# New durations in the planner that orders a fused attention and MLP kernel

## The chip, the cores and the metric

The kernel runs on one core of a Trainium2 chip. The metric is the device time of one execution in microseconds (us), and lower is better. TensorE is called PE here and its weight loads PEld; VectorE is DVE, ScalarE is ACT, GpSimd is POOL, and SyncE, which issues the DMAs, is SP.

## The reference, cut to what matters

```python
# q, k, v: 4 batches x 8 heads x 576 tokens x 64, float32
scores = (q @ k.T) / 8
thresh = scores.max(-1) - tau
scores = where(scores >= thresh, scores, -1e9)
attn   = exp(scores - scores.max(-1))
attn   = attn / (attn.sum(-1) + 1e-9)
x = (attn @ v)             # laid out as 2304 tokens x 512
h = x @ w_in               # 512 -> 2048            (first MLP)
x = (h * sigmoid(h)) @ w_out   # 2048 -> 512
out = ((x @ w_a) * (x @ w_b)) @ w_out2   # 512 -> 1536 -> 512   (second MLP)
```

## The kernel before

The work is cut into tasks, and a planner (class `Plan`) puts them in order. Every task has an engine, a cost in ns, a rank (lower goes first), tasks that it needs, and buffers that it takes from rings of a given size. The planner runs a clock of its own: whenever an engine is idle it gives it the ready task of lowest rank, and a task becomes ready when those that it needs have ended by their costs plus a lag (`LAG`, and `MORE` by the engine that receives). The order that comes out is written down, engine by engine, and on the chip each engine works through its list in that order and waits where something is not there yet. The costs do nothing else: no instruction depends on them but one kind, the fills (below).

**Attention** is 144 tiles of 128 query rows in 32 groups: for each batch and each pair of heads a group of four tiles (256 tokens, buffer `pa`) and one of five (320 tokens, `pb`). A tile runs: scores on PE into `sa` or `sb` (L516, L523); `lowest` on DVE (L532, the scaled copy and its minimum); `threshold` on DVE (L538, L540); `exp` on ACT (L544, L546); `mask` on DVE with the row sum (L549); four or five transposes on PE (L581) into `tp` or `hb`; and copies out of PSUM on ACT (L588). Per group follow the value products on PE (L626) into `av`, and a copy on ACT into `x` (L647). The row sums go out to DRAM and come back (L651, L658), GpSimd divides piece by piece (L661), and the result is stored (L665). There is one buffer `x`, so the copy L647 of a group waits for the store L665 of the group before. The first 16 tiles ("early") keep their scores in PSUM; from tile 54 on, q and k are first split in two parts (L441 on ACT, L444 on DVE, L447 on POOL).

**Weights of the first MLP** come as 32 chunks of raw words, which are put together in seven steps: two casts on ACT (L343, L348), two operations on DVE (L354, L359), an addition (L364, four pieces on POOL in the first 16 chunks, DVE after), a cast on ACT (L368) and a subtraction on DVE (L372). One buffer `wc` and two `wt`, `wraw` hold one to two chunks at a time.

**The first MLP** is 112 units: 5 blocks of 256 tokens with 16 units each and 2 blocks of 512. A unit is 12 matmuls up (L754) into PSUM bank `hb`, a tanh on ACT (L764), a gate on DVE (L767), two halves (L770 on ACT, L773 on DVE), and 12 matmuls down (L814), one unit later. Its rank is 1000 and more, so it fills what attention leaves of PE. From the sixty-sixth unit on, once attention has ended, a second bank `hc` takes every other unit; until then a unit can only begin when the gate of the one before has freed `hb`. Where PE waits before a transpose, the planner writes fills: transposes of the identity (L579), as many as 0.6 of its planned gap divided by 109 ns, at most 16.

**Weights of the second MLP** are prepared once attention has ended (lines 877 to 912, rank 1e6, so they take what is left of ACT and DVE); then the second MLP runs (L1127, L1213).

Of the kernel before, what the change touches and what calls it, by code (L numbers as in the profile page):

```python
# [20 lines left out]
B, H, S, D = 4, 8, 576, 64  # L21
# [8 lines left out]
NH = S // 2  # L30
# [26 lines left out]
R_T, R_AV, R_EV, R_NORM = 2, 3, 1, -2  # L57
# [21 lines left out]
class Plan:  # L79
# [8 lines left out]


    LAG = {"PE": 200, "DVE": 125, "ACT": 140, "Pool": 70, "none": 0}  # L90
    MORE = {"PE": 110, "Pool": 40}

    PIPE, LAND = 330, 1300
    WINDOW = 3413
# [108 lines left out]
def act_ns(n, psum=False, scalar=False):  # L203
    return int(n / 1.2 + (50 if psum else 93) + (93 if scalar else 0))


def dve_ns(n, fast=False):
    return int(n / (1.92 if fast else 0.96) + 67)


def pool_ns(n):
    return int(2.35 * n + 90)


def pieces(n, most):
# [5 lines left out]
def pe_ns(n):  # L221
    return int(n * 0.4375 + 7)
# [3 lines left out]
def fused_kernel(ctx: ExitStack, tc: tile.TileContext, qk, qk2, v, tau, w_in, w_out, w_a, w_b, w_o2, out):  # L226
# [10 lines left out]
    pl = Plan()  # L237
# [58 lines left out]
    scale = const.tile([P, 1], F32, name="scale")  # L296
# [30 lines left out]
    wt, w_ready = {}, {}  # L327

    def split_weight(key, src, rank, dst, after=(), lo_engine="Pool", scale_engine="DVE", most=512, total_engine="Pool"):
# [5 lines left out]
        s = {}  # L335
# [34 lines left out]
        def lo(o):  # L370
# [2 lines left out]
                              op=ALU.subtract)  # L373

        a = dma(rank, P * 4096, load, take=["wraw"], behind=after)
        l = pl.add("ACT", act_ns(512), rank, low, [a], take=["wt"])
        c = pl.add(scale_engine, act_ns(512) if scale_engine == "ACT" else 335, rank, scale, [a], take=["wc"],
                   port=scale_engine == "DVE")
        h = pl.add("DVE", 335, rank, sign, [a, c], port=True)
        j = pl.add("DVE", dve_ns(512), rank, join, [h, c], port=True)  # L380
# [31 lines left out]
    def add(engine, cost, rank, fn, after=(), take=(), behind=(), **kw):  # L412
        t = pl.add(engine, cost, rank, fn, after, take, behind, **kw)
        att_tasks.append(t)
        return t
# [54 lines left out]
    def inverses(n, m):  # L470

        s = {}

        def guard():
            nc.vector.tensor_scalar(out=s["sum"][:, :m], in0=s["sum"][:, :m], scalar1=EPS, scalar2=None, op0=ALU.add)

        def inverse():  # L480
            nc.vector.reciprocal(out=sums[:, :m], in_=s["sum"][:, :m])

        def total(k):
            def fn():
                if "sum" not in s:
                    s["sum"] = sm_p.tile([P, 5], F32, name="sum", bufs=2)
                return s["sum"][:, k:k + 1]
            return fn

        def finish(masked):  # L490
            gd = add("DVE", 150, n + R_NORM, guard, masked)
            return add("DVE", 150, n + R_NORM, inverse, [gd], ["rs"])

        return total, finish

# [2 lines left out]
    def softmax(parts, total):  # L498
# [4 lines left out]
        s = {}  # L503
# [46 lines left out]
                                           op0=ALU.is_ge if early else ALU.is_le, op1=ALU.mult, accum_out=total())  # L550
            s["e"] = s["e"].rearrange("p a n -> p (a n)")

        cost = 4 * pe_ns(NH) * len(parts) if parts[0][0]["split"] else 780
        s["scored"] = add("PE", cost, n, scores, [t for hd, *_ in parts for t in hd["ready"]], [bank])
        lw = add("DVE", dve_ns(S) + 75, n, lowest, [s["scored"]], ["e"] if early else ["e", "t"])
        th = add("DVE", 190, n - 0.5, threshold, [lw])
        ex = add("ACT", act_ns(S, early, True) + 30, n, exp, [lw])
        s["ready"] = add("DVE", dve_ns(S) + (110 if early else 80), n - 1, mask, [ex, th], port=not early)
        if early:
            pl.free(bank, s["ready"])  # L560
        else:
# [6 lines left out]
    def weigh(b, half, c, tiles, v, last):  # L568
# [53 lines left out]
        def values(ks):  # L622

            for k in ks:
                for h in range(2):
                    nc.tensor.matmul(s["av"][h * D:(h + 1) * D, :nq], lhsT=v["v"][:, h, k], rhs=s["p"][:, k, h * nq:(h + 1) * nq],  # L626
                                     start=(k == 0), stop=(k == 4), skip_group_check=True)
# [8 lines left out]

        av = ts
        for ks in AV_PARTS:
            av = add("PE", 2 * len(ks) * (int(nq / 1.2) + 47) + 100, last_n + R_AV, lambda ks=ks: values(ks),
                     [*(left if 4 in ks else full), v["ready"]], behind=[av])  # L640
        pl.free(buf, av)
        if last:
# [716 lines left out]
```

## Time and profile before

| | us |
|---|---|
| three runs: lowest, median, highest | 1123.73, 1124.1, 1127.24 |
| the profiled execution, its own time | 1128.0 |
| its span, first to last instruction | 1125.9 |
| PE busy (matmuls) | 1095.8 |
| DVE busy | 832.2 |
| ACT busy | 571.4 |
| POOL busy | 160.9 |

Busy shares are of the whole span. They say little by themselves, since the stages differ: attention with weight preparation up to about 200 us, attention beside the first MLP up to about 500 us, the rest of the first MLP up to about 690 us, then the second MLP. A matmul's time in the trace is from its start until its result is there; matmuls overlap, so what one takes of PE is the distance from its start to that of the next.

### The profile page before, as it was taken

The page shows a single profiled execution, that of the slowest core. Times are in us where ns is not written, and L with a number is a line of the kernel's source. Part 1 is how long each engine was busy: PE and PEld are TensorE (multiplying, and loading weights), DVE is VectorE, ACT ScalarE, POOL GpSimd, SP SyncE. Part 2 cuts the span into 40 slices and gives each one's busy share as a digit, 9 for nine tenths or more (in the row PEclk, how much of TensorE's full clock was granted, in tenths as well). Part 3 has the DMA queues.
Part 4 walks back from the last instruction along what each step waited for, and adds up shares of the span by engine and source line. Part 5 has one row for each costly group of instructions (what it writes and reads, how often), then busy time and mean ns, then how long its engine had stood idle before and what let it go on. Part 6 is the DMA issues. An engine that isn't in the chain of part 4 may idle for free.

```text
span 1125.9 us, 19426 instructions
## 1 busy us (share of the span) xinstructions
PE 1095.8 (97%) x7086; PEld 979.4 (87%) x7086; DVE 832.2 (74%) x1722; ACT 571.4 (51%) x1012; POOL 160.9 (14%) x306
## 2 busy tenths in 40 slices
PE   8889989999999999999999999999999999999998
PEld 6557857899888888899988888899999999999998
DVE  7878998777777777748998987766884668536664
ACT  6877776667666676646665654411242114401132
POOL 2443111333422243312000000000000000000000
PEclk9989999999999999999999999999999999999999
DMA  5654642323322232128998789798889888888882
GB/s 185 202 168 146 187 159 71 119 78 95 104 81 76 82 98 82 34 69 265 300 316 268 258 270 346 258 298 255 253 310 308 251 260 246 281 281 254 254 254 76
DMA packets 114975, 222.27 MB, mean 197 GB/s; under 512 B 8112, under 2 KB 75328, under 8 KB 114880
## 3 DMA queue, kind: packets, MB, share of 16 engines
q1 hardware_dynamic: 114736, 221.03, 61.5%
q8 instruction: 56, 0.92, 0.3%
q14 instruction: 39, 0.32, 0.1%
q10 hardware_dynamic: 144, 0.00, 0.0%
HBM read 173.74 MB, written 47.26 MB: 196 GB/s over the span
## 4 chain that ended last, share of the span: by engine, by line
PE 62%; DMA 0%; ACT 0%; DVE 0%; POOL 0%; issue 0%; ACTq 0%
PE pr L1127 23%; PE pr L1213 12%; PE hb L754 7%; PE hc L754 5%; PE sb L814 4%; PE yd L814 2%; PE yc L814 2%; PE yf L814 2%; PE ye L814 2%; PE av L626 1%; PE tp L581 1%; PE sa L516 1%; DMA xT_d<-x 0%; DVE tm L1072 0%; PE av L631 0%; ACT pb L588 0%
## 5 line engine op out<-in xcount | busy, mean ns | idle before, releaser
L1127 PE MATMUL pr<-w 128*128 128x384 f32 x1512 | 262.8, 334 | 0.0
L1127 PEld LDWEIGHTS pr<-w 128*128 128x128 f32 x1512 | 262.3, 188 | 0.2
L754 PE MATMUL hb<-xh,w 128*128 128x256 f32 (+1 forms) x704 | 156.2, 313 | 1.8 <-DVE th L767 1.2
L532 DVE TENSOR_SCALAR_CACHE_REDUCE t<-sa,nscale 128x576 f32<-128x576 f32 x128 | 103.7, 810 | 53.5 <-PE sa L516 46.7
L1213 PE MATMUL pr<-zh,w 128*128 128x384 f32 x504 | 128.3, 336 | 0.0
L549 DVE SCALAR_TENSOR_TENSOR e<-t,thr,e 128x576 f32<-128x576 f32 x128 | 109.8, 859 | 20.4 <-ACT e L546 18.9
L754 PEld LDWEIGHTS hb<-xh,w 128*128 128x128 f32 x704 | 114.4, 192 | 11.2 <-issue 1.6
L581 PE MATMUL tp<-ident,e 128*128 128x128 f32 x706 | 107.4, 279 | 17.0 <-DVE e L549 8.2
L581 PEld LDWEIGHTS tp<-ident,e 128*128 128x128 f32 x706 | 79.2, 141 | 41.6 <-issue 16.1
L546 ACT ACTIVATE e<-t,min 128x576 f32<-128x576 f32 x128 | 99.9, 782 | 19.5 <-DVE t L532 18.7
L754 PE MATMUL hb<-xl,w 128*128 128x256 f32 (+1 forms) x352 | 107.4, 305 | 0.7 <-POOL xl L723 0.7
L814 PE MATMUL sb<-gh,w 128*128 128x256 f32 (+1 forms) x576 | 98.6, 301 | 0.0
L1213 PEld LDWEIGHTS pr<-zh,w 128*128 128x128 f32 x504 | 91.1, 188 | 0.0
L814 PEld LDWEIGHTS sb<-gh,w 128*128 128x128 f32 x576 | 80.4, 190 | 6.6 <-issue 2.9
L1213 PE MATMUL pr<-zl,w 128*128 128x384 f32 x252 | 84.7, 336 | 0.0
L1139 ACT COPY yo<-pr 128x384 f32<-128x384 f32 x18 | 8.6, 480 | 123.4 <-PE pr L1127 123.4
L754 PEld LDWEIGHTS hb<-xl,w 128*128 128x128 f32 x352 | 67.3, 191 | 3.7 <-POOL xl L723 0.9
L516 PE MATMUL sa<-sp 128*128 128x288 f32 (+1 forms) x400 | 70.4, 302 | 0.0
L661 POOL TENSOR_TENSOR x<-x,xi 128x128 f32<-128x128 f32 (+2 forms) x80 | 41.6, 544 | 190.3 <-DMA xi<-r_d 88.9
L978 ACT CAST zh<-z 128x768 fp32r<-128x768 f32 x45 | 37.6, 836 | 61.1 <-PE pr L1213 38.7
L588 ACT COPY pb<-tp 128x512 f32<-128x512 f32 (+2 forms) x128 | 59.8, 493 | 11.9 <-PE tp L581 11.2
L447 POOL TENSOR_TENSOR sp<-qk,sp 64x115 fp32r<-64x115 f32 (+1 forms) x100 | 58.0, 611 | 52.2 <-issue 36.6
(142 smaller groups left out, 1977.6 us busy)
## 6 DMA issues: line engine op xcount, KB each, us to landing
w<-wab_d SPq DMA_DIRECT2D x126, 512.0 KB
w<-wo_d SPq DMA_DIRECT2D x63, 512.0 KB
wab_d<-uw SPq DMA_DIRECT2D x18, 896.0 KB
qk<-qk SPq DMA_DIRECT2D x20, 576.0 KB
wo_d<-uw SPq DMA_DIRECT2D x10, 896.0 KB
wraw<-w_in SPq DMA_DIRECT2D x16, 512.0 KB
wraw<-w_out SPq DMA_DIRECT2D x16, 512.0 KB
v<-v SPq DMA_DIRECT2D x20, 320.0 KB
```

Source lines behind the costliest of these rows:

```text
L447: nc.gpsimd.tensor_tensor(out=s["t"][D:, 0, o], in0=s["r"][D:, o], in1=s["t"][D:, 0, o].bitcast(F32), op=ALU.subtract)
L516: nc.tensor.matmul(s["s"][:r + m, j, :NH], lhsT=hd["t"][:, 0, c - r:c + m], rhs=hd["t"][:, k, j * NH:(j + 1) * NH], start=(k == 1), stop=( ...
L532: nc.vector.tensor_scalar(out=s["t"], in0=s["s"][:, :, :NH], scalar1=nscale, scalar2=None, op0=ALU.mult, op1=ALU.min, accum_out=s["min"])
L546: nc.scalar.activation(out=s["e"], in_=s["t"], func=AF.Exp, scale=-1.0, bias=s["min"])
L549: nc.vector.scalar_tensor_tensor(out=s["e"], in0=s["s"][:, :, :NH] if early else s["t"], scalar=s["thr"], in1=s["e"], op0=ALU.is_ge if ear ...
L581: nc.tensor.transpose(t["tp"][:, j * P:(j + 1) * P], e["e"][:, o:o + P], ident)
L588: nc.scalar.copy(out=dst(s["p"]), in_=t["tp"][:, :m * P] if m < 4 else t["tp"].rearrange("p (k q) -> p k q", k=4))
L661: nc.gpsimd.tensor_tensor(out=s["x"][:, o], in0=s["x"][:, o], in1=s["i"][:, o], op=ALU.mult)
L754: nc.tensor.matmul(s["h"], lhsT=w[:, a, o:o + P], rhs=xx, start=(c == 0 and k == 0), stop=(c == NC - 1 and k == 2))
L814: nc.tensor.matmul(ys[j][e // per][:, e % per * tn:(e % per + 1) * tn], lhsT=w[:, a, e * P:(e + 1) * P], rhs=gs[j, f][g], start=(f == 0 an ...
L1127: nc.tensor.matmul(bank[:, m, :TN], lhsT=w["w"][:, 2 * m + k, a], rhs=y[i][x][:, k, :TN], start=(i in (1, 6, 5) and k == 0 and q == 0), st ...
L1213: nc.tensor.matmul(bank[:, c, :TN], lhsT=w["w"][:, 2 * e + c, a], rhs=z[x][:, e], start=(i in (1, 6, 5) and sl == 0 and e == 0 and q == 0) ...
```

## The change

Ten numbers that the planner reckons with are replaced. No instruction of the kernel is changed by hand, and no rank, ring or lag but `MORE["Pool"]`.

```diff
-    MORE = {"PE": 110, "Pool": 40}
+    MORE = {"PE": 110, "Pool": 110}
...
 def pool_ns(n):
-    return int(2.35 * n + 90)
+    return int(2.5 * n + 95)
...
-        l = pl.add("ACT", act_ns(512), rank, low, [a], take=["wt"])
-        c = pl.add(scale_engine, act_ns(512) if scale_engine == "ACT" else 335, rank, scale, [a], take=["wc"],
+        l = pl.add("ACT", 565, rank, low, [a], take=["wt"])
+        c = pl.add(scale_engine, 565 if scale_engine == "ACT" else 335, rank, scale, [a], take=["wc"],
...
-            gd = add("DVE", 150, n + R_NORM, guard, masked)
-            return add("DVE", 150, n + R_NORM, inverse, [gd], ["rs"])
+            gd = add("DVE", 100, n + R_NORM, guard, masked)
+            return add("DVE", 90, n + R_NORM, inverse, [gd], ["rs"])
...
-        cost = 4 * pe_ns(NH) * len(parts) if parts[0][0]["split"] else 780
+        cost = 4 * pe_ns(NH) * len(parts) if parts[0][0]["split"] else 850
...
-        th = add("DVE", 190, n - 0.5, threshold, [lw])
-        ex = add("ACT", act_ns(S, early, True) + 30, n, exp, [lw])
-        s["ready"] = add("DVE", dve_ns(S) + (110 if early else 80), n - 1, mask, [ex, th], port=not early)
+        th = add("DVE", 126, n - 0.5, threshold, [lw])
+        ex = add("ACT", 725 if early else 680, n, exp, [lw])
+        s["ready"] = add("DVE", dve_ns(S) + 77, n - 1, mask, [ex, th], port=not early)
...
-            av = add("PE", 2 * len(ks) * (int(nq / 1.2) + 47) + 100, last_n + R_AV, lambda ks=ks: values(ks),
+            av = add("PE", 2 * len(ks) * (int(nq / 1.2) + 3) + 90, last_n + R_AV, lambda ks=ks: values(ks),
```

In ns this makes of the old costs: a raw cast (`act_ns(512)`) 519 to 565; a POOL piece of 128 columns 390 to 415; guard 150 to 100 and inverse 150 to 90; scores of an unsplit tile 780 to 850; threshold 190 to 126; early exp 653 to 725, late exp 696 to 680; early mask 777 to 744, late mask 747 to 744; the value products of a group of 256 columns 2800 to 2340, and of 320 columns 3330 to 2870.

What this does to the lists is shown at three places. The first is DVE's list from its thirty-first mask (L549) on, in the stage in which weights are still put together (L354, L359, L364, L372 are weight steps, L767 and L773 belong to the first MLP). Before:

```order
L549 SCALAR_TENSOR_TENSOR e,sum<-t,thr,e 128x576
L532 TENSOR_SCALAR t,min<-sa,nscale 128x576
L372 TENSOR_TENSOR w<-wt,w 128x512
L354 TENSOR_SCALAR wraw<-wraw 128x512
L540 TENSOR_SCALAR thr<-min,tadd 128x1
L359 SCALAR_TENSOR_TENSOR wc<-wc,wraw 128x512
L549 SCALAR_TENSOR_TENSOR e,sum<-t,thr,e 128x576
L364 ISA wt<-wc,wt 128x1024
L532 TENSOR_SCALAR t,min<-sa,nscale 128x576
L372 TENSOR_TENSOR w<-wt,w 128x512
L767 SCALAR_TENSOR_TENSOR th<-th,hb 128x256
L354 TENSOR_SCALAR wraw<-wraw 128x512
```

The same place, from the thirty-first mask on, in the changed kernel's list of DVE:

```order
L549 SCALAR_TENSOR_TENSOR e,sum<-t,thr,e 128x576
L773 TENSOR_TENSOR gl<-th,gh 128x256
L540 TENSOR_SCALAR thr<-min,tadd 128x1
L532 TENSOR_SCALAR t,min<-sa,nscale 128x576
L549 SCALAR_TENSOR_TENSOR e,sum<-t,thr,e 128x576
L540 TENSOR_SCALAR thr<-min,tadd 128x1
L532 TENSOR_SCALAR t,min<-sa,nscale 128x576
L549 SCALAR_TENSOR_TENSOR e,sum<-t,thr,e 128x576
L372 TENSOR_TENSOR w<-wt,w 128x512
L354 TENSOR_SCALAR wraw<-wraw 128x512
L540 TENSOR_SCALAR thr<-min,tadd 128x1
L359 SCALAR_TENSOR_TENSOR wc<-wc,wraw 128x512
```

Weight steps moved back against attention. Over the whole list the seventeenth chunk is ready (L372) after 29 masks before and after 35 now, and the last after 43 before and 48 now.

The second place is ACT's list around the copy L647 of the twenty-seventh group (128x384, that is 256 tokens and the sums). Before:

```order
L588 COPY pa<-tp 128x256
L764 ACTIVATE th<-hb 128x256
L546 ACTIVATE e<-t,min 128x576
L770 CAST gh<-th 128x256
L647 COPY x<-av 128x384
L588 COPY pb<-tp 128x4x128
L441 CAST sp<-qk 128x1152
L588 COPY pb<-tp 128x4x128
L588 COPY pb<-tp 128x256
```

The same copy, with what stands around it, in the changed kernel's list of ACT:

```order
L588 COPY pa<-tp 128x256
L770 CAST gh<-th 128x256
L546 ACTIVATE e<-t,min 128x576
L441 CAST sp<-qk 128x1152
L546 ACTIVATE e<-t,min 128x576
L647 COPY x<-av 128x384
L588 COPY pb<-tp 128x4x128 x2
L588 COPY pb<-tp 128x256
```

The cast L441 and one more exp moved ahead of the copy that waits for the `x` buffer; the copies out of `tp` behind it stayed.

The third place is DVE's list after attention's last mask, where the first MLP runs on alone (L836 empties the sums of a block; L883 to L909 prepare weights of the second MLP; `hc` in place of `hb` shows the second bank). Before, from the last two gates of small units on the one bank:

```order
L767 SCALAR_TENSOR_TENSOR th<-th,hb 128x256
L773 TENSOR_TENSOR gl<-th,gh 128x256
L767 SCALAR_TENSOR_TENSOR th<-th,hb 128x256
L773 TENSOR_TENSOR gl<-th,gh 128x256
L836 TENSOR_SCALAR yo<-sb 128x512
L767 SCALAR_TENSOR_TENSOR th<-th,hc 128x256
L773 TENSOR_TENSOR gl<-th,gh 128x256
L767 SCALAR_TENSOR_TENSOR th<-th,hb 128x256
L883 TENSOR_SCALAR ur<-ur 128x512
```

A part of the same stretch, between two gates on the one bank, in the changed kernel's list of DVE:

```order
L767 SCALAR_TENSOR_TENSOR th<-th,hb 128x256
L901 TENSOR_TENSOR us<-us 128x256
L888 SCALAR_TENSOR_TENSOR us<-us,ur 128x512
L773 TENSOR_TENSOR gl<-th,gh 128x256
L897 TENSOR_TENSOR us<-us 128x128
L894 ISA us<-us 128x1024
L897 TENSOR_TENSOR us<-us 128x128
L901 TENSOR_TENSOR us<-us 128x256
L767 SCALAR_TENSOR_TENSOR th<-th,hb 128x256
```

Attention ends earlier in the list: in PE's order 732 up matmuls (61 units) stand ahead of its last value product before, and 630 (52 and a half units) now. The second bank still begins with the sixty-sixth unit, so 12 units on one bank follow attention now, against 4, and weight steps stand between the last seven of their gates, where none stood before.

## Rows read from the trace of the kernel before

**Rows 1.** Five stretches: busy us and instructions of each engine, granted clock, DMA.
```profile
0.00:100.00 100.00, 83.81 (x555) 55.77 (x556) 80.10 (x215) 74.31 (x138) 40.53 (x90) 0.95 0.58 175
100.00:150.00 50.00, 48.76 (x363) 38.31 (x363) 48.01 (x117) 39.91 (x81) 6.91 (x12) 1.00 0.58 178
150.00:200.00 50.00, 45.83 (x343) 33.93 (x342) 40.42 (x109) 33.72 (x70) 7.08 (x12) 1.00 0.31 101
200.00:500.00 300.00, 295.95 (x2388) 264.29 (x2387) 218.67 (x614) 196.89 (x381) 96.99 (x175) 0.99 0.26 81
500.00:1126.00 626.00, 621.49 (x3446) 587.15 (x3444) 445.05 (x669) 226.55 (x346) 9.36 (x19) 1.00 0.82 266
```

**Rows 2.** PE's waits, 0 to 200 us: us in total, times, longest.
```profile
PE tp L581 <- DVE e L549: 8.2, 10, 1.9
PE sa L523 <- DVE t L532: 4.1, 7, 1.5
PE tp L581 <- ACT pb L588: 3.3, 3, 1.5
```

**Rows 3.** ACT's waits, 0 to 200 us, for the weights.
```profile
ACT w L368 <- DVE wt L364: 6.8, 9, 2.3
ACT w L368 <- POOL wt L364: 4.8, 8, 1.7
```

**Rows 4.** Timeline of DVE: start, us, instruction, count; in brackets idle before it.
```profile
104.34 0.21 DVE L540 TENSOR_SCALAR thr<-min,tadd 128x1 f32<-128x1 f32 x1
104.47 0.68 DVE L364 CUSTOM_DVE_ANT_0 wt<-wc,wt 128x1024 uint16<-128x1024 uint16 x1
```

**Rows 5.** Timeline of POOL, four pieces of one chunk.
```profile
61.03 1.69 POOL L364 TENSOR_TENSOR wt<-wc,wt 128x128 uint32<-128x128 uint32 x4 [3.94 <-DVE wc L359]
```

**Rows 6.** Timelines of ACT, SP, POOL and PE, 184 to 200 us.
```profile
184.06 0.53 ACT L647 COPY x<-av 128x448 f32<-128x448 f32 x1 [1.01 <-PE av L626]
187.03 0.51 SPq L658 DMA_DIRECT2D xi<-r_d  x1
192.57 1.66 POOL L661 TENSOR_TENSOR x<-x,xi 128x106 f32<-128x106 f32 x3 [11.69 <-DMA xi<-r_d]
194.26 0.33 SPq L665 DMA_DIRECT2D xT_d<-x  x1
198.19 0.48 ACT L647 COPY x<-av 128x384 f32<-128x384 f32 x1 [2.68 <-DMA xT_d<-x]
199.21 0.44 PE L581 MATMUL tp<-ident,e 128*128 128x128 f32 x2 [1.20 <-ACT pb L588]
```

**Rows 7.** Waits of ACT and of PE, 200 to 500 us.
```profile
ACT x L647 <- DMA xT_d<-x: 18.5, 8, 4.3
PE tp L581 <- ACT pb L588: 4.1, 3, 1.9
```

**Rows 8.** Timeline of ACT and PE at 311 us, and the stretch behind it.
```profile
310.82 0.48 ACT L647 COPY x<-av 128x384 f32<-128x384 f32 x1 [4.32 <-DMA xT_d<-x]
311.84 0.33 PE L581 MATMUL tp<-ident,e 128*128 128x128 f32 x1 [1.94 <-ACT pb L588]
312.90:316.30 3.40, 3.40 (x17) 3.40 (x17) 2.64 (x6) 2.15 (x4) 2.58 (x5) 0.50 0.10 33
```

**Rows 9.** Timeline: a unit of the first MLP on one bank, attention over.
```profile
497.02 0.28 PE L754 MATMUL hb<-xl,w 128*128 128x256 f32 x1
497.75 0.42 DVE L767 SCALAR_TENSOR_TENSOR th<-th,hb 128x256 f32<-128x256 f32 x1 [1.56 <-ACT th L764]
498.58 0.40 PE L754 MATMUL hb<-xh,w 128*128 128x256 f32 x2
```

**Rows 10.** Timeline: a unit on two banks beside weight preparation.
```profile
543.10 0.28 PE L754 MATMUL hb<-xl,w 128*128 128x256 f32 x1
544.36 1.08 DVE L909 TENSOR_TENSOR uw<-us,uw 128x896 fp32r<-128x896 f32 x1
545.36 0.41 DVE L767 SCALAR_TENSOR_TENSOR th<-th,hb 128x256 f32<-128x256 f32 x1
```

## The prediction

> **What bounds the kernel now.** I read three views in this order. First the table of stretches [rows 1]: PE is busy in nearly all of the time, and what is left, its idle time, lies in front: 16.2 us before 100 us, 1.2 and 4.2 us in the next two stretches, 4.05 us in the 300 us after them, and 4.5 us in the last 626 us, nearly all of it the store behind the last matmul. The change can't touch what PE has to compute (it orders the same matmuls, the fills apart), so all that it can win is some 25 us of PE's idle time, and all that it can lose is new idle time. From 500 us on PE stands so densely that nothing is to be had there. Second the waits of PE before 200 us [rows 2]: it waits for masks (8.2 us), for the score bank to come free (4.1 us) and for copies out of PSUM (3.3 us), never for DMA. These are links of the softmax chain on DVE and ACT. Third the waits of PE from 200 to 500 us [rows 7]: three waits of together 4.1 us, all for the copy out of `tp`, and above them ACT's eight waits of together 18.5 us in L647, for the one `x` buffer. So two things hold PE up: before 200 us the softmax chain and the weights share DVE and ACT, and after it the round of the `x` buffer sometimes stops ACT in front of a copy that PE needs.
>
> **The numbers themselves.** Each engine's list is fixed, so a cost that is wrong shows as a wait of one engine for another that the plan thought done. The threshold takes 0.13 us of DVE from its start to the next start [rows 4], not 190 ns, and a POOL piece 0.41 us (1.69 us for four, the last one counted whole, [rows 5]), not 390 ns. The new numbers are nearer for an undisturbed instruction. They are not the durations of a disturbed one: three pieces of 106 columns took 1.66 us at 192.57 us [rows 6], where the new formula says 360 ns each, together 1.08.
>
> The Trainium skill ("SBUF — State Buffer", section "Who interferes with whom") says that a DVE operation with two SBUF inputs and a GpSimd operation that reads SBUF exclude each other for a whole instruction. The 1.66 us agree with it. By that rule the corrected piece is right only between masks, and the plan stays short wherever both run; this gives the rival "no gain" below.
>
> **First term, the fills.** The order has 87 fills in place of 80. At the 109 ns that the kernel itself divides by, that is 7 x 0.109 = +0.8 us if all lie on PE's path, and 0 if each only fills a wait. I take +0.8.
>
> **Second term, before 200 us.** ACT waits 6.8 + 4.8 us for weight chunks that DVE and POOL haven't added up yet [rows 3]; behind the waiting cast stand exps and copies that PE needs. The plan thought a chunk ready too soon: 2 x 46 ns for the casts, 4 x 25 ns for the pieces and 70 ns of lag, some 0.26 us in each of the 16 chunks with POOL pieces. Now it knows, and weight steps stand later: the last chunk comes after 48 masks, not 43. That evens the load. DVE is busy 48.0 of 50 us from 100 to 150 us and 40.4 of 50 after it [rows 1], since the weights run out there, while PE waits in both. Counted in the two orders by start-to-start times, DVE has in the five groups from the seventh to the eleventh 18, 24, 15, 21 and 7 us of work before, and 15, 16, 20, 19 and 19 us now; PE has 90 us of work over these groups in both. I take it that half of PE's 5.4 us of idle time between 100 and 200 us goes, -2.5 us rounded, and of the 16.2 us before it, where both orders place 67 fills in planned gaps, only -1.0. Together -3.5 us. The bounds: at best two thirds of the waits of [rows 2] go, 15.6 x 2/3 = -10 us; at worst DVE, now loaded evenly beside PE, makes the 100 us stretch 5 us longer, +5 us (DVE's 88.4 us of work in it become 93 with the weight steps that moved in from before, and each engine waits for the other).
>
> **Third term, 200 to 500 us.** Between the value products of a five-tile group and those of the next four-tile group PE's order now holds about 12.0 us of work (20 transposes, 24 score and 34 MLP matmuls, 10 value products with two passes each) where it held 11.2, and on the other half 12.5 where it held 16.2. The round of the `x` buffer took 14.1 us at its late example: from the copy at 184.06 over the load at 187.03, the pieces at 192.57 and the store at 194.26 to the next copy at 198.19, for which ACT waited 2.68 us and PE behind it 1.20 us [rows 6]. On the half that waits now the plan leaves 0.8 us more, so each of the three waits of [rows 7] shrinks by about 0.7 us: -2.0 us. Of what is queued behind the stopped copy, a cast of the heads and an exp have moved ahead of it; the copies for PE remain. Bounds: all of 4.1 us and the slow stretch below gone, -5.8 us; on the other side two late rounds now also stop the half that was cut from 16.2 to 12.5 us, 2 x (14.1 - 12.5) = +3 us.
>
> At 312.90 us a stretch of 3.4 us ran at a granted clock of 0.50, which is 1.2 of the two levels 1.2 and 2.4 GHz, with PE busy throughout; ahead of it ACT had waited 4.32 and PE 1.94 us [rows 8]. It cost half of its length, 1.7 us. I count it only in the bound.
>
> The Trainium skill ("TensorE: Matmul & The Clock Gate", section "What's actually happening") has the slow level as the default that activity releases. The row agrees, slow right behind a wait. By the rule the stretch goes with the wait, and the third term would be -3.7, not -2.0.
>
> **Fourth term, the first MLP alone on one bank.** The last matmul up of a unit started at 497.02 us, its gate ended at 498.17, and the next unit began at 498.58 without a wait [rows 9]: 0.41 us of slack, as only 12 matmuls down stand between. Weight preparation can eat that. With two banks the gate at 545.36 us came behind a subtraction of 1.08 us and ended 2.67 us after the last matmul up at 543.10 [rows 10]; on one bank the next unit would have begun 2.67 - 1.56 = 1.1 us late. That is the latest of the 15 units from 505 to 546 us; four of them end past the slack, 0.12 us on the mean of 15. The new order has seven gates on one bank among weight steps: 7 x 0.12 = +0.9 us, between 0 and 7 x 1.1 = +7.7.
>
> **Sum.** +0.8 - 3.5 - 2.0 + 0.9 = -3.8 us. Against the profiled execution's own 1128.0 us (2.1 us outside its span) that is 1124.2. This execution lies 3.9 us above the median of the runs, so I set the difference against the median: 1124.1 - 3.8 = 1120.3 us.
>
> **The rivals.** *No gain.* The waits are set by what the new numbers leave out (collisions, DMA rounds), and only places change. For it: the 1.66 us of [rows 6], and that a DMA round, not a repriced cost, lies behind ACT's 18.5 us. Against it: the 11.6 us of [rows 3] are just what was mispriced. Second and third term go, the rest stays: 1124.1 + 1.7 = 1125.8.
>
> *Slower: the one `x` buffer becomes the bound.* Both halves of a pair now have 12.0 to 12.5 us of PE work, against a round of 14.1 us at its longest. If six of the 22 rounds after 200 us are that late and none is hidden, they cost 6 x 1.75 = +10.5 us, and the time is 1120.3 + 10.5 = 1131. It decides once rounds are longer than 12.5 us as a rule. Against it: only three PE waits in 300 us so far, and DVE has 81 us of slack there [rows 1].
>
> *Slower: DVE bounds 100 to 200 us.* The second term is then +5 in that stretch in place of -2.5, 1120.3 + 7.5 = 1128. Against it: PE's work beside it is no larger.
>
> **How the numbers follow.** A measurement of this kernel tells about 0.3% (3.4 us) from no change; faster means under 1120.7. Chances: a gain as summed 0.44, with its own range 1112 to 1120.7; no gain 0.35; the `x` buffer 0.13; DVE 0.08. So faster 0.44, same 0.35, slower 0.21. The range goes down to 1112 (second and third term halfway to their best ends) and up to 1130, which leaves out most of the `x` buffer case.
>
> **What would show it.** Right: ACT's waits in L368 before 200 us fall under 6 us, PE's idle time from 100 to 200 us to about 3 us; PE's waits for `pb` copies after 200 us total under 3 us; attention's last value product comes some 25 us earlier; between it and the second bank a few waits of PE for the gate L767, under 2 us. Wrong: ACT's waits in L647 grow past 25 us with PE waits behind them, or DVE is busy over 96% from 100 to 200 us while PE's idle time there grows.

## The result: 0.7% slower

The changed kernel takes 1133.26 us (median of 4 runs, 1132.11 to 1133.34), the kernel before 1123.91 on the same chip (4 runs, 1122.91 to 1127.24). The ratio of the comparison is 1.0068, with a 95% interval of 1.0042 to 1.0094; the quotient of the two medians, 1.0083, lies inside it. The forecast was 1120.3, within 1112 to 1130, so both the direction and the range were wrong. The profiled executions lie only 5.2 us apart (spans 1131.1 and 1125.9 us), because that of the kernel before is 4.1 us above its median. The traces can explain these 5.2 us, not all of the 9.4 between the medians. A second pair of traces with the same orders (e13 and e5 below) lies 6.6 us apart.

The table of stretches of the changed kernel answers to [rows 1] (from and to, length, then busy us and instructions of PE, PEld, DVE, ACT, POOL, the granted clock, DMA). Its last row ends 5.1 us before this kernel does; in the kernel before it runs to the end.

```profile
0.00:100.00 100.00, 86.27 (x564) 56.19 (x565) 82.16 (x222) 74.21 (x137) 39.79 (x83) 0.95 0.59 174
100.00:150.00 50.00, 46.84 (x354) 36.78 (x354) 42.05 (x110) 37.90 (x77) 10.30 (x22) 1.00 0.52 158
150.00:200.00 50.00, 45.55 (x319) 33.32 (x316) 43.01 (x106) 34.96 (x69) 6.01 (x9) 0.93 0.41 126
200.00:500.00 300.00, 296.81 (x2381) 262.86 (x2380) 230.88 (x627) 203.57 (x390) 112.48 (x193) 0.99 0.30 94
500.00:1126.00 626.00, 626.00 (x3481) 591.49 (x3481) 437.35 (x660) 223.01 (x339) 0.00 (x0) 1.00 0.81 259
```

Two rows matter. From 150 to 200 us PE begins 319 matmuls where it began 343, and its granted clock is 0.93, not 1.00. From 100 to 150 us DVE is busy 42.05 us in place of 48.01, and PE is busy 1.9 us less: DVE was relieved, and PE gained nothing.

The busy time itself misleads here. Over the whole span PE is busy 6.4 us more than before (1095.8 us), and its idle time fell from 30.1 to 28.9 us, although the kernel is slower. The busy times of the changed kernel over its whole span:

```profile
PE 1102.2 (97%) x7093; PEld 981.0 (87%) x7093; DVE 836.4 (74%) x1722; ACT 573.7 (51%) x1012; POOL 168.6 (15%) x306
```

The one row over the stretch that decides, 150 to 250 us, first of the kernel before:

```profile
150.00:250.00 100.00, 95.83 (x744) 78.46 (x743) 77.59 (x212) 67.23 (x133) 25.05 (x43) 1.00 0.33 105
```

The same stretch of the changed kernel:

```profile
150.00:250.00 100.00, 93.25 (x683) 74.01 (x679) 81.76 (x213) 68.32 (x132) 25.92 (x41) 0.95 0.37 117
```

To compare kernels I worked out PE's lost time: from each matmul's start to the next, less that distance where the same shape runs densely (119.5 ns for 128x256, 233 for 512 columns, and so on); fills and slow clock count as lost. Before, 62.1 us in all; after, 67.3. The difference is the 5.2 us of the spans. This measure sees what the idle time does not: matmuls that count as busy but stand further apart, or run at the slow clock.

What ACT waited for at the two casts of a weight chunk, 0 to 200 us, in the changed kernel ([rows 3] has the two L368 rows of before):

```profile
ACT wt L343 <- DMA wraw<-w_in: 9.6, 7, 3.2
ACT wt L343 <- DMA wraw<-w_out: 5.5, 6, 3.0
ACT w L368 <- DVE wt L364: 3.5, 4, 1.4
ACT w L368 <- POOL wt L364: 2.1, 3, 1.4
```

The rows at L343 in the kernel before, same stretch:

```profile
ACT wt L343 <- DMA wraw<-w_in: 3.9, 4, 1.2
ACT wt L343 <- DMA wraw<-w_out: 0.5, 2, 0.4
```

The waits at L368 fell from 11.6 to 5.6 us, as forecast. But those for the raw words at L343 rose from 4.4 to 15.1. Together these two waits take 20.7 us of ACT in place of 16.0 (22.4 and 19.4 with L343's waits for DVE, 1.7 us after and 3.4 before). Two of the waits for raw words and what stood behind them, first on ACT, then SP, then PE (start, us, instruction; in brackets the idle time before it):

```profile
161.02 0.66 ACT L343 ACTIVATE wt<-wraw 128x512 uint32<-128x512 uint32 x1 [1.72 <-DMA wraw<-w_in]
163.40 0.78 ACT L546 ACTIVATE e<-t,min 128x576 f32<-128x576 f32 x1
165.82 0.67 ACT L343 ACTIVATE wt<-wraw 128x512 uint32<-128x512 uint32 x1 [1.64 <-DMA wraw<-w_in]
...
161.48 0.33 SPq L665 DMA_DIRECT2D xT_d<-x  x1
161.91 0.37 SPq L339 DMA_DIRECT2D wraw<-w_in  x1
...
165.50 0.77 PE L581 MATMUL tp<-ident,e 128*128 128x128 f32 x5 [1.47 <-DVE e L549]
167.78 0.79 PE L754 MATMUL hb<-xh,w 128*128 128x256 f32 x2 [0.78 <-DVE w L372]
```

The exp L546 stood behind the waiting cast, the mask behind the exp, and the transposes L581 behind the mask; at 167.78 us a unit of the first MLP waits for its chunk. From there PE runs slowly although it has work. The whole slow stretch, and the part of it in which PE has no gap:

```profile
167.10:173.90 6.80, 5.90 (x22) 3.02 (x24) 6.80 (x18) 4.97 (x9) 0.00 (x0) 0.50 0.32 106
171.00:174.00 3.00, 3.00 (x14) 1.42 (x12) 3.00 (x7) 1.83 (x3) 0.00 (x0) 0.52 0.24 96
```

A granted clock of 0.50 is the lower of the two levels (1.2 GHz). The last chunk is ready (end of L372) at 191.8 us; before, at 177.1. At 210 us a second round stops ACT in front of PE's copies, the reload of `qk`. The chain of waits that ends there (start, us, what):

```profile
203.89 0.92 POOL sp L447
204.82 0.02 issue
204.83 4.06 DMA qk<-qk
208.89 0.02 issue
208.91 1.15 ACT sp L441
```

The copy for PE behind that cast, and PE's wait for it:

```profile
210.28 0.85 ACT L588 COPY pb<-tp 128x256 f32<-128x256 f32 x2
210.70 0.33 PE L581 MATMUL tp<-ident,e 128*128 128x128 f32 x1 [2.04 <-ACT pb L588]
```

PE loses 2.04 us, and slow clock follows here too:

```profile
211.50:214.90 3.40, 3.40 (x14) 1.48 (x13) 2.58 (x7) 1.23 (x3) 1.90 (x4) 0.50 0.12 39
```

From 150 to 250 us the kernel before ran at a clock of 1.00 throughout. The lost time that falls into these two slow stretches is 5.7 us, most of the 8.6 us by which the changed kernel loses more from 150 to 250 us. The clock is not all of it: in a second profile of the changed kernel (e5) it is 3.6 us, and e10 and e12 lose 13.2 and 13.9 us there at a clock of 1.00.

After this the change does what was forecast. The rows of the changed kernel that answer to [rows 7], 200 to 500 us:

```profile
ACT x L647 <- DMA xT_d<-x: 7.2, 7, 2.2
PE tp L581 <- ACT pb L588: 2.0, 1, 2.0
```

The one wait for `pb` copies that PE has left there is the one at 210.70; five waits for masks (1.1 us) are new. The slow stretch of [rows 8] is gone.

### The profile page after: what moved, and what is told of

Read it like the earlier page. It is cut to its first block, busy times and chain, and to the rows that moved or that the text cites. A ratio compares the mean times of both kernels' runs of the same rounds, so it can differ in the third digit from the quotient of the medians.

```text
span 1131.1 us, 19481 instructions
## 1 busy us (share of the span) xinstructions
PE 1102.2 (97%) x7093; PEld 981.0 (87%) x7093; DVE 836.4 (74%) x1722; ACT 573.7 (51%) x1012; POOL 168.6 (15%) x306
## 4 chain that ended last, share of the span: by engine, by line
PE 82%; DMA 7%; DVE 5%; ACT 3%; issue 2%; POOL 1%; SPq 0%; ACTq 0%; DVEq 0%; POOLq 0%
PE pr L1127 23%; PE pr L1213 12%; PE hb L754 10%; PE sb L814 7%; PE av L626 6%; PE hc L754 5%; PE tp L581 5%; PE sa L516 4%; PE yc L814 2%; PE yd L814 2%; PE ye L814 2%; PE yf L814 2%; DMA wraw<-w_in 2%; DMA wraw<-w_out 2%; DMA xi<-r_d 1%
## 5 line engine op out<-in xcount | busy, mean ns | idle before, releaser
L549 DVE SCALAR_TENSOR_TENSOR e<-t,thr,e 128x576 f32<-128x576 f32 x128 | 111.8, 874 | 17.1 <-ACT e L546 14.3
L581 PE MATMUL tp<-ident,e 128*128 128x128 f32 x706 | 107.0, 280 | 11.7 <-DVE e L549 8.3
L546 ACT ACTIVATE e<-t,min 128x576 f32<-128x576 f32 x128 | 99.6, 781 | 28.6 <-DVE t L532 28.1
L581 PEld LDWEIGHTS tp<-ident,e 128*128 128x128 f32 x706 | 79.5, 142 | 36.8 <-issue 19.1
L814 PE MATMUL sb<-gh,w 128*128 128x256 f32 (+1 forms) x576 | 94.3, 299 | 0.0
L661 POOL TENSOR_TENSOR x<-x,xi 128x128 f32<-128x128 f32 (+2 forms) x80 | 44.7, 582 | 178.8 <-DMA xi<-r_d 78.0
L773 DVE TENSOR_TENSOR gl<-th,gh 128x256 fp32r<-128x256 f32 (+1 forms) x112 | 61.4, 549 | 8.8 <-ACT gh L770 8.6
L447 POOL TENSOR_TENSOR sp<-qk,sp 64x115 fp32r<-64x115 f32 (+1 forms) x100 | 60.5, 636 | 48.2 <-ACT sp L441 36.2
```

Of the source, the lines that this page charges most:

```text
L447: nc.gpsimd.tensor_tensor(out=s["t"][D:, 0, o], in0=s["r"][D:, o], in1=s["t"][D:, 0, o].bitcast(F32), op=ALU.subtract)
L546: nc.scalar.activation(out=s["e"], in_=s["t"], func=AF.Exp, scale=-1.0, bias=s["min"])
L549: nc.vector.scalar_tensor_tensor(out=s["e"], in0=s["s"][:, :, :NH] if early else s["t"], scalar=s["thr"], in1=s["e"], op0=ALU.is_ge if ear ...
L581: nc.tensor.transpose(t["tp"][:, j * P:(j + 1) * P], e["e"][:, o:o + P], ident)
L773: nc.vector.tensor_sub(out=s["gl"], in0=s["t"], in1=s["gh"].bitcast(F32))
L814: nc.tensor.matmul(ys[j][e // per][:, e % per * tn:(e % per + 1) * tn], lhsT=w[:, a, e * P:(e + 1) * P], rhs=gs[j, f][g], start=(f == 0 an ...
```

## The experiments

### One table

Each experiment was timed in five rounds against the kernel before. Lost time is in us, from one profile each; `last` is when the last weight chunk is ready.

| kernel | ratio (95%) | 0–150 | 150–250 | 250–500 | last |
|---|---|---|---|---|---|
| before | 1 | 40.7 | 9.5 | 11.6 | 177 |
| e13, same lists as before | 1.0000 (0.9982–1.0017) | 41.1 | 9.0 | 10.6 | 178 |
| changed | 1.0068 (1.0042–1.0094) | 40.3 | 18.1 | 7.9 | 192 |
| e5, changed again | 1.0081 (1.0056–1.0106) | 41.4 | 16.1 | 9.0 | 191 |
| e1 early part new | 1.0044 (1.0028–1.0059) | 40.5 | 15.3 | 7.8 | 195 |
| e2 late part new | 1.0015 (1.0004–1.0026) | 39.6 | 8.9 | 8.8 | 175 |
| e3 changed, step 1.1 | 1.0062 (1.0048–1.0077) | 40.4 | 13.9 | 7.8 | 186 |
| e4 before, step 1.5 | 1.0038 (1.0024–1.0052) | 42.2 | 12.6 | 5.6 | 190 |
| e6 norm alone | 0.9982 (0.9964–1.0000) | 36.3 | 11.3 | 7.7 | 180 |
| e7 weight prices | 1.0088 (1.0066–1.0110) | 45.7 | 15.9 | 8.4 | 191 |
| e9 casts alone | 0.9993 (0.9976–1.0011) | 40.6 | 8.9 | 11.1 | 178 |
| e10 POOL alone | 1.0024 (1.0005–1.0042) | 40.0 | 13.2 | 7.3 | 185 |
| e11 all but weights | 1.0039 (1.0022–1.0056) | 39.8 | 13.9 | 8.6 | 189 |
| e12 weights cheaper | 1.0051 (1.0033–1.0069) | 44.7 | 13.9 | 7.7 | 188 |
| e14 changed + lag | 0.9974 (0.9959–0.9990) | 40.4 | 10.6 | 5.6 | 188 |
| e18 its stores early | 0.9991 (0.9973–1.0008) | 41.2 | 10.5 | 5.4 | 189 |
| e15 before + lag | 0.9963 (0.9949–0.9977) | 40.6 | 9.6 | 6.1 | 180 |
| e16 norm + lag | 0.9981 (0.9964–0.9998) | 43.6 | 11.6 | 5.5 | 185 |

Three pairs have the same lists of PE, DVE, ACT and POOL: before and e13, changed and e5, e14 and e18. They agree within 2 us in each column and about 1 us in the sum, so these columns belong to the lists as long as SP's transfers come at much the same time; e17 below has the changed kernel's lists too, with SP's order altered, and loses far more. The totals do not order kernels that lie a few tenths of a per cent apart: the profile of before lies 4.1 us above its median.

### Which part of the change, and which stretch

```diff
# e1: the new weight costs everywhere, the new attention costs for the first 45 tiles, as here
+        th = add("DVE", 126 if n < 45 else 190, n - 0.5, threshold, [lw])
# e2: the old weight costs, the new attention costs from tile 45 on
+        th = add("DVE", 126 if n >= 45 else 190, n - 0.5, threshold, [lw])
```

> The new durations for the weight casts and POOL, and the new attention durations for the first 45 of the 144 tiles only; the later tiles keep the old ones. DVE's list up to the tenth group is that of the changed kernel (the seventeenth weight chunk after 35 masks, the last after 48), attention ends after 60 units, nearly as before. Late-weights theory (the loss is made before 250 us, where weight chunks come later than before and PE and ACT wait): all of the loss without the gain that the changed kernel has after 250 us, 1133 + 3 = 1136 us, between 1133 and 1139. Rival, packed attention (the loss is made where the attention of batches 2 to 4 is squeezed between fewer MLP matmuls): nearly that of before, 1124 to 1127 us.

> The old durations for weight casts, POOL and the first 45 tiles, the new attention durations from tile 45 on. The lists up to the tenth group are those of before; attention ends after 54.5 units as in the changed kernel. Late-weights theory: the changed kernel's gain between 250 and 500 us (3.7 us of PE's lost time in the two traces) without its loss: 1120 us, between 1118 and 1122. Packed attention: the whole loss, 1130 to 1134 us.

e1 has most of the loss, with 15.3 us lost from 150 to 250 us. e2 has none of that loss, and from 250 to 500 us it loses 2.8 us less than the kernel before. Its time does not show that gain (1.0015). The profile of before is of an execution 4.1 us above its median, that of e2 of one 0.6 us above, so the two columns don't compare median with median; more is not known.

```diff
# e3, on the changed kernel; e4, on the kernel before, with 1.5
-    W_AT, W_STEP = 2, 1.3
+    W_AT, W_STEP = 2, 1.1
```

> All new durations, but the rank step from one weight chunk to the next is 1.1, not 1.3, so that weights go ahead of attention: the seventeenth chunk stands after 31 masks (29 before, 35 in the changed kernel), the last after 46 (43 and 48); attention ends after 53.5 units, as packed as in the changed kernel. Late-weights theory: about two thirds of the loss gone, 1124 to 1128 us. Packed attention: no change, 1132 to 1135 us.

> All old durations, but the rank step from one weight chunk to the next is 1.5, not 1.3: the last chunk stands after 50 masks (43 before), attention ends after 59 units. Nothing else. Late-weights theory: the loss comes from this alone, 1130 to 1136 us. Packed attention: as before, 1123 to 1126 us.

`W_STEP` spaces the ranks of the weight chunks. Ranking them earlier brought the last chunk from 192 to 186 us and won next to nothing in time. Ranking them later in the kernel before brought it to 190 us and cost 0.4%, with all costs old.

```diff
# e5: the changed kernel, unaltered
# e6: of the change, guard and inverse alone
+            gd = add("DVE", 100, n + R_NORM, guard, masked)
+            return add("DVE", 90, n + R_NORM, inverse, [gd], ["rs"])
# e7: the three weight costs alone
+    MORE = {"PE": 110, "Pool": 110}
+    return int(2.5 * n + 95)
+        l = pl.add("ACT", 565, rank, low, [a], take=["wt"])
...
```

> The changed kernel itself, beside the other three, on the chip that they run on. The comparisons so far gave 1.0068 for it and 1.0044 for the early half of the change; every theory expects 1.006 to 1.009 of before here, and it is the measure for the three others.

> One edit alone: guard 150 to 100 and inverse 150 to 90 ns, two instructions in each of the 32 groups. DVE's list then has the seventeenth weight chunk after 33 masks (29 before) and the last after 48 (43), attention ends after 59.5 units (61). Late-weights theory: most of the loss of the early half, 1.003 to 1.005 of before, with waits of ACT for raw weights (L343) over 8 us between 100 and 250 us. Theory that the sum of all repriced tasks packs attention: next to nothing, 0.999 to 1.001.

> The new durations of the casts and of POOL alone, the attention tasks keep the old ones. The last chunk stands after 44 masks (43 before), the seventeenth after 31 (29), attention ends after 61.5 units. If the loss came from the dearer weight steps themselves: 1.004 to 1.007. Late-weights theory (only where the chunks end up counts): 0.999 to 1.002.

The loss repeats in e5. In e6 the chunks stand further back in the order, yet it is not slower: the place in the order does not decide. e7 holds the whole loss, with attention's costs untouched. That looked like the cause, so the next four runs took the weight costs apart.

```diff
# e9: the cast alone.  e10: the POOL piece and its lag alone.  e11: everything but these two.
# e12: the kernel before with the three weight costs moved the other way
+    MORE = {"PE": 110, "Pool": 0}
+    return int(2.2 * n + 85)
+        l = pl.add("ACT", 473, rank, low, [a], take=["wt"])
...
```

> The kernel before, with only the raw-weight cast repriced from 519 to 565 ns. The seventeenth chunk and the last are ready after 29 and 43 masks, as in the kernel before. Theory (dearer weight steps make the plan start each next chunk later, chunks arrive later in real time, and PE starves before 200 us): the three weight edits together made 1.0088; this is 46 of the roughly 260 ns per chunk that they add, twice, so about a third: 1.003, and the last chunk is ready between 178 and 190 us. Rival (the loss does not follow the price: any other order comes out anywhere between 0.998 and 1.009): no forecast, but no link between the time and how late the chunks are.

> The kernel before, with only the GpSimd piece (390 to 415 ns for 128 columns) and its lag (40 to 110 ns) repriced. The seventeenth chunk and the last are ready after 33 and 48 masks, against 29 and 43. Theory (dearer weight steps deliver chunks later in real time): the larger part of the 1.0088 of the three edits, 1.005 to 1.009, last chunk ready after 188 us, as in all slower kernels so far (186 to 197, against 175 to 180 in the faster ones). Rival (order lottery): no link.

> The changed kernel with the old costs of casts, GpSimd pieces and GpSimd lag; all attention costs stay new. The last chunk comes after 49 masks. Theory (the weight prices carry the loss): within 0.998 to 1.002 of the kernel before, since the loss of 1.0068 to 1.0081 goes with the edits left out, and the last chunk is ready by 182 us. Rival (losses add up over any part of the change; early attention costs alone with the weights gave 1.0044): 1.003 to 1.006.

> The kernel before, with the weight steps priced the other way, by as much as the change raises them: cast 473 in place of 519 ns, GpSimd piece 366 in place of 390, GpSimd lag 0 in place of 40. Theory (dearer is later is slower): not slower than the kernel before, 0.996 to 1.001, and the last chunk ready at 180 us or earlier. Rival (order lottery, or the old prices stand at an optimum by tuning): slower by 0.3% or more, also with chunks that come no later than before.

That reading falls. The parts do not add up (0.9993 and 1.0024, together 1.0088), everything but them also loses, and cheaper weights lose 0.5%. A price moved down lost as a price moved up did. What the losers have in common is the table's last column and the 150 to 250 us one: a last chunk at 185 us or later goes with 12.6 to 18.1 us lost there, one at 175 to 180 us with 8.9 to 11.3. The kernels with the lag, below, are the exception. ACT's waits for raw words at L343 before 200 us go with the loss in all of them better. The eight kernels with 14.3 to 18.6 us of them (changed, e1, e4, e5, e7, e10, e12, e16) lose 53.2 to 61.6 us before 250 us, the first two columns added. Eight with 4.4 to 13.0 us lose 47.6 to 51.7. Only e3 and e11 don't fit (10.9 and 10.3 us, 54.3 and 53.7 lost). That is a link over kernels, not a test.

### The queue of SP, and the round of the x buffer

```diff
# e8, on the changed kernel; the scratch of the DMAs is raised as well
-            nc.sync.dma_start(out=xT_d[c, :, t0:t0 + nq], in_=s["x"][:, :nq])
+            nc.gpsimd.dma_start(out=xT_d[c, :, t0:t0 + nq], in_=s["x"][:, :nq])
...
-    nc = bacc.Bacc("TRN2", target_bir_lowering=False, num_devices=1, dynamic_dma_scratch_size=64)
+    nc = bacc.Bacc("TRN2", target_bir_lowering=False, num_devices=1, dynamic_dma_scratch_size=512)
```

> The changed kernel with one DMA issued from another engine: the store of x (L665) by GpSimd right behind its division, not by SP. The lists of PE, DVE and ACT are the same as in the changed kernel. Theory that weight loads come late because they stand on SP's queue behind stores that wait for GpSimd: ACT's waits for raw weights (12.3 us between 100 and 250 us) fall under 5 us, and a third to a half of the loss goes, 1.003 to 1.005 of before. If the lateness is in the lists of DVE and ACT: as the changed kernel, 1.006 to 1.009.

e8 came out at 1.0196 (1.0168 to 1.0225). Issued from POOL, the store holds its engine 588 ns (median of 32), where SP's issue takes 327; ACT's L647 waited 16.2 us behind those stores. It moved the cost and settled nothing about SP.

```diff
# e13, on the kernel before: two transfers per raw chunk, one line in place of one
-            nc.sync.dma_start(out=s["raw"], in_=src)
+            [nc.sync.dma_start(out=s["raw"][:, c], in_=src[:, c]) for c in ((slice(0, 256), slice(256, 512)) if key[0] in ("in", "out") else (slice(0, 512),))]
# e14 on the changed kernel, e15 on the kernel before, e16 on e6: a planned lag
-                        n["at"] = max(n["at"], done + lag)
+                        n["at"] = max(n["at"], done + lag + (1600 if e == "Pool" and n["engine"] == "SP" else 0))
```

> The kernel before with the same plan and the same lists of PE, DVE, ACT and POOL; only each raw-weight chunk of the first MLP is fetched by two transfers of half the columns, one behind the other on SP, in place of one. This makes the chunks physically later while no order changes. Theory A (late chunks are a cause: PE's list was laid out for chunks that come at a certain time, and each us that they come later is lost before 200 us): the last chunk, at 177 us in the kernel before, is ready at 183 us or later, and the time rises by 0.3 to 0.6%. Theory B (late chunks are only a symptom of an engine order in which ACT and DVE stop often): the last chunk is later by as much, and the time stays within 0.15%.

> The changed kernel, with 1600 ns more of planned lag from a GpSimd task to an SP transfer that needs it, so that the plan puts the stores L665 further back in SP's list, behind weight loads that could go before them. In the changed kernel SP waited 40.0 us for GpSimd in front of L665 from 70 to 220 us, against 27.1 before. Theory A1 (the weight loads stand behind those stores, and this makes the chunks late): SP's waits at L665 fall under 15 us in that stretch, the last chunk is ready by 185 us in place of 191, and the loss of 0.7 to 0.8% falls to 0.4% or less. Rival (the stores don't decide, the order of the casts on ACT and DVE does): last chunk still after 187 us, ratio 1.005 or more.

> The kernel before, with the same 1600 ns of planned lag between GpSimd and the transfers that need it, all other numbers old. Theory A1: SP's waits at L665 (27.1 us from 70 to 220 us) fall by half, last chunk by 178 us, and the time is 0.997 to 1.001 of the kernel before. Rival (any re-drawn order loses against this one): 1.003 or more.

> The kernel before with the new costs of guard and inverse alone (0.9982 in an earlier run, the fastest so far) and the 1600 ns of lag: a candidate to beat both kernels. Theory A1: 0.995 to 0.999. Rival (re-drawn orders come out anywhere): 1.002 to 1.006, with the last chunk after 185 us.

e13 told nothing apart: the two half transfers did not make the chunks later (178 us). ACT's waits for raw words rose from 4.4 to 7.1 us in it, and nothing was lost. Whether late chunks are a cause by themselves was therefore not shown with the order held fixed.

The lag of 1600 ns won twice: e14 is 0.9974 in place of 1.0068, and e15 0.9963, the lowest ratio of all, though its interval overlaps those of e14, e16 and e6. On e6 it changed nothing (e16, 0.9981 for 0.9982). But not by the theory: e14's last chunk still comes at 188 us. ACT's wait for the store from 200 to 500 us tells why. In e14:

```profile
ACT x L647 <- DMA xT_d<-x: 0.6, 1, 0.6
```

That row was 18.5 us before [rows 7], and 7.2 in the changed kernel; in e15 it is 1.6, and PE's wait for `pb` copies is gone in e14, e15 and e16. The plan now knows that the round of the `x` buffer is longer and puts L647 further back in ACT's list. Copies for PE still stand right behind it in e15, but it hardly waits any more. For e15 that stretch is the whole gain: from 250 to 500 us it loses 5.5 us less, in the two columns in front of it the same within 0.1 us, after 500 us some 1 us more, and the medians lie 3.5 us apart. The lag is not the only way there: e4, with old costs and no lag, loses as little from 250 to 500 us (5.6). ACT still waits 10.7 us at L647 there, but PE only 0.3 us for `pb` copies. e14 also loses 7.5 us less than the changed kernel from 150 to 250 us. The lag reaches every SP transfer that waits for POOL, the reload of `qk` behind L447 too, and e14 has no wait at L441 for it there; which share that has wasn't tested.

Two runs part the place of the stores on SP from the lists that the lag drew for the other engines.

```diff
# e17: the changed kernel's lists; before they are written down, on SP alone:
+    for t in [t for t in order if t["fn"].__qualname__.endswith("weigh.<locals>.store")]:
+        order.remove(t)
+        i = 0
+        while order[i]["start"] <= t["start"] + 4800 and not any(order[i] is u for u in t["next"] + t["first"]):
+            i += 1
+        order.insert(i, t)
# e18: e14's lists; on SP alone each store moved forward to just behind the POOL work it needs
```

> The changed kernel with the very lists of PE, DVE, ACT and POOL that it has; on SP alone each store L665 is moved back as far as the first task that needs it (at most 4.8 us of planned time), which puts it behind one more load of q, v or raw weights in 8 of the first 9 groups, as the planned lag of 1600 ns did in the kernel at 0.9974. Theory S (the place of the stores in SP's list decides): the loss of 0.7 to 0.8% falls to 0.3% or less. Rival R (what the lag did was to draw new lists for PE, ACT and DVE, and those decide): 1.005 or more.

> The kernel with the new costs and 1600 ns of lag that came out at 0.9974, with its very lists of PE, DVE, ACT and POOL; on SP alone each store L665 is put forward again to just behind the GpSimd work that it waits for, in front of the one or two loads that the lag had let pass. Theory S: half or more of what the lag won is lost again, 1.002 or more. Rival R: within 0.2% of the kernel with the lag, 0.996 to 0.9995.

e17 came out at 1.0407 (1.0374 to 1.0439). Of its lost time 35.1 us lie between 250 and 500 us (7.9 in the changed kernel), and its last chunk comes at 197 us. Its waits from 200 to 500 us:

```profile
PE tp L581 <- ACT pa L588: 21.4, 7, 3.5
...
ACT x L647 <- DMA xT_d<-x: 41.0, 9, 5.9
```

So a store that goes later on SP, on lists laid out for an early one, stops ACT in front of L647 and PE behind ACT. e18 keeps e14's lost time in every column, though SP there waits for POOL in front of the stores longer than in any other kernel looked at: 47.0 us from 70 to 220 us, where the changed kernel waits 40.0 and e14 25.5. So the waits of SP's queue are not what costs in e14 and e18; the lists of the other engines decide. Theory S is refuted, rival R stands. Which place in those lists decides, that of L647 or that of the casts on ACT, is read from the waits and was not tested one by one.

## Why the prediction was wrong, by its own steps

**The premise: this step failed.** The prediction says of the change that "all that it can lose is new idle time". PE's idle time fell from 30.1 to 28.9 us, and the kernel became slower. In e13 and e5 it is 29.6 and 30.4 us, while the spans lie 6.6 us apart. Nearly all of the loss lies inside what the rows call busy: slow clock, and short waits that the overlap of matmuls hides (one of 256 columns counts 0.28 us, while the next can begin 0.12 us after it).

**First term, the fills: the count right, the cost open.** 87 for 80, as counted. Their +0.8 us was not measured by itself; it is contained in the figures below.

**Second term, before 200 us: this step failed.** Forecast −3.5 us, found 48.9 us lost before and 52.4 after, +3.5 (e13 to e5 about +3). Its first half held: the waits at L368 went from 11.6 to 5.6 us. The failing step is "weight steps stand later", and of it "That evens the load". DVE was evened (42.05 and 43.01 us busy in the two stretches, where it was 48.01 and 40.42), but DVE's load was not what held PE. ACT waits in order, and it only waited one step earlier, for raw words whose transfer no edit repriced: +10.7 us at L343 against −6.0 at L368. And the stage of the weights runs 15 us longer, so that these stops stand beside attention until 192 us. I read the later chunks as relief and priced no harm in them; over the table they go with the loss. The exchange of one wait for the other is shown. That it alone costs the 3.5 us is not: e9 has much of it (11.0 us at L343, 6.3 at L368) and loses nothing before 250 us. The sign that the prediction named came out against it: PE's idle time from 100 to 200 us was to fall from 5.4 to 3 us, and rose to 7.6. A second mistake lies under it: I took truer costs of a few tasks for a truer plan. e7, e9, e10, e11 and e12 show that new costs drew the lists anew each time, and that redrawn lists without the lag come out between 0.998 and 1.009, whichever way the costs moved.

**Third term, 200 to 500 us: the direction right, the place too wide.** From 250 to 500 us the loss fell by 3.7 us (1.6 from e13 to e5), for −2.0 forecast. The waits of PE for `pb` copies there did not shrink by 0.7 us each, they went. The loss in this stretch also fell in e7, e10 and e12 with attention's costs untouched (7.3 to 8.4 us lost, for 11.6), so the new attention costs were not needed for it. The Trainium skill ("TensorE: Matmul & The Clock Gate", section "What's actually happening") has the slow level as the default that activity releases. By it the prediction set −3.7 beside its −2.0, the slow stretch going with the wait. The changed kernel agrees, but that is in part luck, for e13, with the lists of before and 3.7 us of the same waits, has no slow stretch there either (250 to 500 us, clock 1.00, 10.6 us lost):

```profile
250.00:500.00 250.00, 245.86 (x1995) 219.19 (x1995) 182.24 (x513) 163.11 (x317) 82.14 (x146) 1.00 0.24 76
```

But from 200 to 250 us the round of `qk` cost 4.7 us (1.3 to 6.0), a place that this term didn't look at, so the whole is +1.0.

**Fourth term, the MLP alone on one bank: right.** +0.9 forecast; the loss after 500 us went from 0.3 to 1.1. About 0.5 us of it are three units that begin late at 500.4, 503.3 and 506.3 us, among the weight steps. In the changed kernel the last L647 starts at 472.19 us, before at 491.95, 20 us earlier for 25 forecast.

**The sum.** The second term came out 7.0 us above its forecast and the third 3.0; together they make the miss of the traces (−3.8 forecast, +5.2 found, the fills contained). Both stay inside the bounds given for them (+5 and +3 us), but by luck: neither DVE nor late rounds of the `x` buffer made the loss. The range's lower end was also reckoned wrong: halfway to the best ends of the second and third term gives 1115, not 1112. It had no part in the miss.

**The rivals.** The slower ones were the wrong ones. ACT's waits for the `x` buffer fell to 7.2 us, and DVE was nowhere near its bound. The mechanism that the rows show, a wait of ACT for raw weights in the place of the one removed, had its first rows in the kernel before (4.4 us at L343) and no price of its own. "No gain" came nearest: it said that the waits are set by DMA rounds and collisions and only change places, but it allowed no harm beyond +1.7 us.

**What stays open.** That late chunks themselves cause the loss from 150 to 250 us is a link over many kernels, not shown with the order held fixed; e14 (188 us, 10.6 us lost) speaks against its being all. The same holds for the waits at L343. Of the 9.4 us between the medians, 4.1 are in no trace: no execution of the kernel before near its median of 1123.9 us was kept.

## What to carry to other kernels

In a fixed order laid out by a planner, ask of each repriced task which wait comes one link further up the same chain, and price the rounds through DMA first: here one lag for a round that the plan thought too short gave 0.37%, while the corrected durations cost 0.7%. A cost that is nearer to the trace does not by itself give a better order; any change of costs draws another one, so time several neighbours (some prices up, some down) before a result is laid to the price. An instruction that may wait for a transfer costs what stands behind it on its engine. And don't forecast from idle time alone: here PE's idle time fell while the kernel lost 5.2 us.

## What the hardware showed that was not expected

A plain store issued by POOL held its engine 588 ns against 327 on SP. The Trainium skill ("DMA: Bandwidth & Descriptors", section "Issuing engine by pattern") names SP for a simple store, and e8 agrees. Two transfers of half a raw chunk in place of one (e13) left the time at 1.0000 and the last chunk at 178 us, for 177.
